# A planner that reckons TensorE's changes of array shape, and all first weights decoded in PSUM

## The chip, the cores and the metric

One core of one Trainium2 chip runs the whole kernel. The metric is the device time of one execution in microseconds (us), the median over several runs.

## The reference

Attention over 4 batches of 8 heads (576 tokens of 64 values) is followed by two feed-forward layers (512 to 2048 to 512) over the 2304 tokens, all in fp32. The attention has two parts that are added: one over pooled tokens (means of four), one local, in which a token sees the tokens at a distance under 4.

```python
def _attn_ref(q, k, v):
    q_d = q.reshape(B, H, Sd, factor, D).mean(axis=3)   # likewise k_d, v_d; factor = 4
    out_d = sm_attn(q_d, k_d, v_d)                      # softmax attention
    out_up = np.repeat(out_d, factor, axis=2)
    mask = np.abs(pos[:, None] - pos[None, :]) < factor
    scores = np.where(mask, scale * q @ k.T, -1e9)
    return out_up + softmax(scores) @ v

x = attn_out.transpose(0, 2, 1, 3).reshape(B * S, H * D)
h = x @ w_in;  x = (h * sigmoid(h)) @ w_out             # first layer
h = x @ w_in2; x = np.where(h > 0, h, np.exp(np.minimum(h, 0)) - 1) @ w_out2
```

## The kernel before

**Stages.** The kernel has an attention stage and a long feed-forward stage. Up to about 44 us TensorE works on batch 0's attention alone, in four pairs of heads. Then the first layer's first half of weights (8 slices of 128 hidden values, each a `w_in` and a `w_out` tile, so 16 weights, `i` from 0 to 15) is applied to the tokens in blocks of 256, as the GEMM units of `unit`: L1077 is the first product (x by `w_in`), L1125 the second (into the block's sums). The attention of batches 1 to 3 runs between these units. Blocks 0 and 1 are interleaved: slices 0 to 3 of block 0, of block 1, then slices 4 to 7 of each, so that both hold their sums at once. Block 2 needs batch 1's attention. Products of fp32 are made of three products of split values (high and low parts, `xh`, `xl`, `wh`, `wl`). Behind the attention stage `paired` runs the remaining passes as long streams of 128x384 and 128x512 products (L1453, L1541, L1543).

**The planner.** The order of instructions on every engine comes from a list scheduler that runs when the program is built. A `Job` has an engine, a duration in us, predecessors, a due time, PSUM banks that it takes (`Hold(banks, kind)`), and for TensorE a `mode`. `pick` finds the job that can start first; among the jobs of its engine that can start within `SLACK` (0.05 us) of it, it takes the one with the earliest due time. `emit` writes its instructions and moves the engine's clock. A job with an `other` engine is put on the one that ends it sooner, with a bias `PREFER`. The planner's durations are estimates; on the chip each engine runs its instructions in the planned order, and waits on semaphores where the plan was wrong. Before the change `STICK` is 0, so a job's shape plays no part, and `mode` knows only "t" (transposes) and "s" (small products); GEMM jobs have none.

**PSUM.** There are eight banks of 128x512 fp32. Kinds are "a" (attention), "h" (result of L1077), "y" (sums of a block, two banks each) and "w" (decoding of weights); at most 3 h, 6 of h and y together, and 2 of w are held at once (`bank_rule`).

**Decoding of a weight** (`decode_jobs`, called by `prepare`): weights land as 128x1024 32-bit words in a `ws` buffer, and come to be an fp32 tile `wf` in these steps: `first` (L411, ScalarE), `half` (L415, ScalarE), `second` (L419, a clamp, VectorE or GpSimd), `third` (L422, a shift and an OR, VectorE), `fourth` (L426, a merge of the sign, VectorE). For `i < N_PSUM` the value between these steps (`temp`) lies in a PSUM bank, else in `wf` itself. `prepare` then splits `wf` into a high part (L1054, ScalarE) and a low one (L1058, GpSimd).

```python
a = Job("A", 0.62, first, list(preds) + [landed[i]], takes=list(takes) + inner, uses=held)
b = Job("V", 0.70 if inner else 0.45, second, [a], other=None if inner or i >= 2 * FP else ("G", 1.1, lambda: second(nc.gpsimd)))
c = Job("V", VEC_[DM], third, [b, a2], port=not inner, uses=held)
```

**Attention** (`attend`, one call per batch and pair of heads): q and k are transposed (L635, full array), the local scores are 40 products of 64x64 (L747), the pooled scores 8 of 64x72 (L800), the pooled output 8 of 72x64 (L892), the local output 40 of 64x64 (L920 in two parts for batches 0 and 1, L958 for 2 and 3). Both softmax results are transposed for their products (L853, L874, "flips"). In the local softmax L766 takes the maxima, L771 subtracts and later scales (GpSimd), L861 copies flips out of PSUM; L839 scales the pooled one. For batch 0 the pooling of v is 44 products (L690). L1105 and L1106 are the first two steps behind a GEMM unit's first product.

**Products of zeros.** `filler` issues TensorE products of zeros (L356) at the start (`WARM`, nine) and, up to the first unit, into every planned gap of TensorE (`fill`). They write into the free bank that came free first.

Of the kernel before, what the change touches and what calls it, by code (L numbers as in the profile page):

```python
# [15 lines left out]
ALU = mybir.AluOpType  # L16
# [6 lines left out]
def attention_moe_moe2_kernel(ctx, tc, q, k, v, wi1, wo1, wi2, wo2, out):  # L23
    nc = tc.nc
# [3 lines left out]
    P = 128  # L28
# [15 lines left out]
    FP = NF // NPASS  # L44
# [8 lines left out]
    WIN = 64  # L53
    WARM = 9
    PREFER = {("G", "V"): 1.5, ("V", "G"): -1.5, ("A", "V"): 0.5, ("V", "A"): -0.5}
    PACKED, PE_POOLED, HALVED, CHUNKED, STICK, T_SECOND = 0, 1, 0, 4, 0.0, 40.0
    BACKLOG = 3.0
    D_ROWS, D_LOCAL, D_V, D_W, S_ROWS, S_LOCAL, X_AFTER = 1.6, 1.9, 1.5, 2.2, 1.1, 2.2, 1
    QUAD_FROM = 2
# [1 line left out]
    LEND = 1  # L61
    SOON, W_EARLY, W_AT = 9.0, 0, -3.0
    LATE, FRAC = 1.0, (0.25, 0.5, 0.75, 1.0)
    SLACK, MOST_H, N_PSUM, SPLIT_F = 0.05, 3, 8, 3
    T_MM, T_FIRST, T_PAIR = 0.1185, 46.0, 6.4
    LAG = 3
    ON_ACT = (0, 2, 3)
# [77 lines left out]
    now = [0.0]  # L145
# [56 lines left out]
    class Job:  # L202
# [61 lines left out]
        def emit(self):  # L264
            t = self.start()
            assert t is not None
            cand.remove(self)
            for h in self.takes:
                h.take()
            if self.eng == "P":  # L270
                if filling[0]:
                    fill(t)
                mode_of[0] = self.mode
                now[0] = t + self.dur
            self.fn()
            clock_of[self.eng] = t + self.dur
            if self.port:
                clock_of["port"] = t + self.dur
            self.end = t + self.dur + self.lat
            if self.dma is not None:  # L280
                clock_of["dma"] = max(clock_of["dma"], t + DMA_WAIT) + self.dma
                self.end = clock_of["dma"] + DMA_LAND + self.safe
            for h in self.uses:
                h.done(self)
            for j in self.after_me:
                j.open_ -= 1
                if not j.open_:
                    blocked.remove(j)
                    cand.append(j)
# [3 lines left out]
    def pick(limit=1e18):  # L293
        best = None
        for job in cand:
            s = job.start()
            if s is not None and s < limit:
                key = (s, job.due, job.serial)
                if best is None or key < best[0]:
                    best = (key, job)  # L300
        if best is None:
            return None
        s = best[0][0] + SLACK
        eng = best[1].eng
        ties = []
        for job in cand:
            if job.eng == eng or job.other and job.other[0] == eng:
                x = job.start()
                if x is not None and x <= s and job.eng == eng:
                    same = eng == "P" and job.mode is not None and job.mode == mode_of[0]  # L310
                    ties.append((job.due - (STICK if same else 0.0), job.serial, job))
        return min(ties)[2] if ties else best[1]

    def pump(t):
# [6 lines left out]
    def run(goals):  # L321
        goals = [j for j in goals if j.end is None]
        while goals:
            job = pick()
            assert job is not None, "stuck"
            job.emit()
            if job in goals:
                goals.remove(job)
# [22 lines left out]

    def filler(n):
        if n > 0:
            entry = min(banks.free, key=lambda x: x[:2])
            for _ in range(n):
                nc.tensor.matmul(entry[2], wz[0][:, :P], wz[0][:, :512], start=True, stop=True)  # L356

    def fill(t):
        gap = t - clock_of["P"]
        if banks.free:  # L360
            filler(min(int((gap - 0.1) / 0.22), 40))

    wz = []

# [26 lines left out]
    def decode_jobs(i, out, preds, takes=(), temp=None):  # L393

        def t():
            return (temp.tile.bitcast(I32) if temp is not None else out())

        def pairs_of(st):
            return st.rearrange("p (n w) -> p n w", w=2)

        held = []
        if i < 2 * FP:
            held = [Hold(WS)]
            wst[i] = held[0]
            landed[i] = Job("S", 0.55, lambda: load_w(i), [], takes=held, dma=D_W, safe=SAFE_W)
        else:
            landed[i] = Job("S", 0.55, lambda: load_w(i), [decoded[i - WS_N]] if i >= 2 * FP + WS_N else [decoded[n] for n in range(2 * FP)], dma=D_W, safe=SAFE_W)

        def first():
            st = pairs_of(wst[i])  # L410
            nc.scalar.activation(t().bitcast(F32), st[:, :, 1].bitcast(F32), AF.Abs, scale=65536.0)  # L411

        def half():
            st = pairs_of(wst[i])
            nc.scalar.activation(st[:, :, 0].bitcast(U32), st[:, :, 0].bitcast(U32), AF.Copy, scale=2.0 ** -29, bias=2.0 ** -10 - 0.5)  # L415

        def second(eng=nc.vector):
            tf = t().bitcast(F32)
            eng.tensor_scalar(tf, tf, 2.0, W_MAX, op0=ALU.max, op1=ALU.min)  # L419

        def third():
            nc.vector.scalar_tensor_tensor(t(), t(), 3, pairs_of(wst[i])[:, :, 0], op0=ALU.logical_shift_left, op1=ALU.bitwise_or)  # L422

        def fourth():
            st = pairs_of(wst.pop(i))
            nc.vector.scalar_tensor_tensor(out(), st[:, :, 1], -(1 << 31), t(), op0=ALU.bitwise_and, op1=ALU.bitwise_or)  # L426

        inner = [temp] if temp is not None else []
        a = Job("A", 0.62, first, list(preds) + [landed[i]], takes=list(takes) + inner, uses=held)
        a2 = Job("A", 0.66, half, [landed[i]], uses=held)  # L430
        b = Job("V", 0.70 if inner else 0.45, second, [a], other=None if inner or i >= 2 * FP else ("G", 1.1, lambda: second(nc.gpsimd)))
        c = Job("V", VEC_[DM], third, [b, a2], port=not inner, uses=held)
        d = Job("V", VEC_[DM], fourth, [c] + ([decoded[i - 1]] if i - 1 in decoded else []), port=not inner, uses=inner + held)
        decoded[i] = d
        return d
# [127 lines left out]
    def attend(i, due):  # L563
# [60 lines left out]
        for n_, cells in enumerate(([(0, c) for c in range(NTB - 1)], [(1, c) for c in range(NTB - 1)], [(0, NTB - 1), (1, NTB - 1)])):  # L624
            bank = Hold(banks, "a")

            def flip(cells=cells, bank=bank):
# [9 lines left out]
            used = {0: [hq], 1: [hk], 2: [hq, hk]}[n_]  # L637
            pj = Job(
                "P", 0.085 * len(cells), flip, [lq] if n_ == 0 else [lk] if n_ == 1 else [lq, lk], lat=0.2,
                takes=[bank] + ([hqk] if n_ == 0 else []), uses=used, mode="t",  # L640
            )
            pj.after(prior)
            prior = [pj]
# [38 lines left out]
        if by_pe:  # L682
# [9 lines left out]
                            start=n == 0, stop=n == len(POOLED_BY) - 1, skip_group_check=True,  # L692
                        )

            psv = Job("P", 1.3, pool_v, [lw], lat=0.2, takes=bankv, uses=[hw, hpool], mode="s")
            for j in range(2):
                dst = lambda j=j: hvd.tile[:HS, 2 * j * D:2 * (j + 1) * D]
                pv.append(alike(
# [30 lines left out]
        def follow(job, key):  # L729
            if key in chain:  # L730
                job.after([chain[key]])
            chain[key] = job
            return job

        for part, (s0, s1, halves_, outs) in enumerate(parts):
# [15 lines left out]
                            start=True, stop=True,  # L751
                        )

            psl = follow(Job("P", 0.15 + 0.11 * (s1 - s0) * 2, scores, copies, lat=0.2, takes=held + ([hE] if start_ else []), uses=[hqk], mode="s"), "psl")
            masked = []
            for j, bank in enumerate(held):
                def add_mask(j=j, bank=bank, s0=s0, s1=s1):
# [37 lines left out]
            def pooled_scores(halves_=halves_, bankd=bankd):  # L795
# [9 lines left out]
                        )  # L805

            psd = follow(Job(
                "P", 0.15 + 0.2 * len(halves_), pooled_scores, [red], lat=0.2, takes=bankd + ([hED, hsm] if start_ else []), uses=[hqkD], mode="s",
            ), "psd")
            exps = []  # L810
            for j, bank in enumerate(bankd):
# [36 lines left out]
            for g0, g1_ in groups:  # L848
# [5 lines left out]
                            bank.tile[:, (s - g0) * P:(s - g0 + 1) * P], E4(s, s + 1).rearrange("p s j w -> p (s j w)"), ident  # L854
                        )

                pj = follow(Job("P", 0.11 * (g1_ - g0), flip, [norm], lat=0.2, takes=[bank] + ([haT] if g0 == 0 else []), uses=[hE], mode="t"), "psE")
                n = (g1_ - g0) * P
                dst = lambda g0=g0, g1_=g1_: aT()[:, g0:g1_, :].rearrange("p s w -> p (s w)")
                flips[g0] = alike(  # L860
# [5 lines left out]
            for a in halves_:  # L866
# [6 lines left out]
                            y_ = x[:, c * HS:(c + 1) * HS] if by_pe else x.rearrange("p (m c) -> p c m", c=2)[:, c, :]  # L873
                            nc.tensor.transpose(bank.tile[:HS, (2 * j + c) * HS:(2 * j + c + 1) * HS], y_, ident[:HS, :HS])  # L874

                pj = follow(Job("P", 0.26, flip, [norm_d], lat=0.2, takes=[bank] + ([haD] if a == 0 else []), uses=[hED], mode="s"), "psD")
                dst = lambda a=a: aD()[:HS, :, a * HS:(a + 1) * HS]
                src = lambda bank=bank: bank.tile[:HS, :4 * HS].rearrange("p (n s) -> p n s", n=4)
                flips_d.append(alike(
# [14 lines left out]
                            start=(c == 0), stop=(c == 1),  # L894
                        )

            psu = follow(Job("P", 0.3 + 0.0015 * (m1 - m0), out_d, flips_d + pv, lat=0.2, takes=[banku], uses=[hvd, haD], mode="s"), "psu")
            ups = alike(
                0.19 + 0.0008 * (m1 - m0),
                lambda banku=banku, m0=m0, m1=m1: nc.scalar.activation(haD.tile[:, m0:m1], banku.tile[:, :m1 - m0], AF.Copy, scale=1.0 / FAC),  # L900
# [8 lines left out]
            if b < QUAD_FROM:  # L909
                for t in outs:  # L910
# [23 lines left out]
                            op=ALU.add,  # L934
                        )

                    pj = Job("P", 0.54, out_l, [lw] + [flips[g] for g in sorted(flips) if t == 1 or g == 0], lat=0.2, takes=[bank], uses=[hw, haT], mode="s")
                    end_ = due[t] if isinstance(due, tuple) else due + 0.5 * t
                    final.append(Job("V", 0.47, join, [pj, ups] + (sum(first_users.values(), []) if b == 1 else second_users if b else []), due=end_, uses=[bank, haD]))
                    x_written[pr, 2 * b + t] = final[-1]  # L940
# [21 lines left out]
                                start=True, stop=True,  # L962
                            )

            pj = follow(Job("P", 0.75, out_l, [lw] + [flips[g] for g in sorted(flips)], lat=0.2, takes=banko, uses=[hw, haT], mode="s"), "pso")
            for t, p0, p1 in ((0, 0, P), (1, 0, D), (1, D, P)):
                bank = banko[t]
                g0 = b * S + t * HALF
# [596 lines left out]
    with tc.manual_schedule():  # L1565
# [51 lines left out]

        for i in range(W_EARLY):
            landed[i].due = W_AT
        filler(WARM)  # L1620
        constants()
        pool_matrix()
# [2 lines left out]
        run(g1_jobs[0, 0])  # L1625
        run(g1_jobs[FILL_TO])
        filling[0] = False
        run([j for b_ in range(B) for j in batch_end[b_]] + list(kept_x.values()) + [x for p_ in w_split.values() for x in p_])
        PREFER.clear()
        attn_pools.close()  # L1630
# [73 lines left out]
```

## Time and profile before

| | |
|---|---|
| median of 3 runs | 893.6 us (892.75 to 894.23) |
| profiled execution, its own time | 893.9 us |
| its span, first to last instruction | 891.5 us |
| TensorE products busy | 875.7 us (98%) |
| VectorE, ScalarE, GpSimd busy | 673.1, 540.8, 273.0 us (76%, 61%, 31%) |
| mean granted clock of TensorE | 0.992 of full speed |

In the profile PE is TensorE's products, PEld its loads of weights, DVE VectorE, ACT ScalarE, POOL GpSimd, SP the engine that issues most DMAs. A busy PE includes the time that products wait in its pipeline. L1077 is line 1077 of the kernel. An operand is named by its tile: `b` is a PSUM bank, `wf` the decoded weight, `ws` its landing buffer, `ring`, `spare` and `yo` the attention's working tiles, `t` the value behind a unit's first product.

### The profile page before, as it was taken

The page shows a single profiled execution, that of the slowest core. Times are in us where ns is not written, and L with a number is a line of the kernel's source. Part 1 is how long each engine was busy: PE and PEld are TensorE (multiplying, and loading weights), DVE is VectorE, ACT ScalarE, POOL GpSimd, SP SyncE. Part 2 cuts the span into 40 slices and gives each one's busy share as a digit, 9 for nine tenths or more (in the row PEclk, how much of TensorE's full clock was granted, in tenths as well). Part 3 has the DMA queues.
Part 4 walks back from the last instruction along what each step waited for, and adds up shares of the span by engine and source line. Part 5 has one row for each costly group of instructions (what it writes and reads, how often), then busy time and mean ns, then how long its engine had stood idle before and what let it go on. Part 6 is the DMA issues. An engine that isn't in the chain of part 4 may idle for free.

```text
span 891.5 us, 17228 instructions
## 1 busy us (share of the span) xinstructions
PE 875.7 (98%) x6614; PEld 817.0 (92%) x6614; DVE 673.1 (76%) x1236; ACT 540.8 (61%) x1226; POOL 273.0 (31%) x278
## 2 busy tenths in 40 slices
PE   9989899999999999999999999999999999999998
PEld 6778798999999999999999999898898998998986
DVE  6899768786967988968848969489489888483562
ACT  4796546664547668648347477286497584571650
POOL 4687977875301211401014213001051031010000
PEclk9999899999999999999999999999999999999999
DMA  9896148551134345154432240350520430220301
GB/s 158 217 220 159 54 107 240 119 143 36 69 95 142 106 142 177 48 201 154 130 112 90 83 155 23 107 178 3 186 71 37 165 131 36 90 89 35 107 1 72
DMA packets 105522, 100.08 MB, mean 112 GB/s; under 512 B 62240, under 2 KB 92448, under 8 KB 105312
## 3 DMA queue, kind: packets, MB, share of 16 engines
q1 hardware_dynamic: 103072, 98.39, 37.2%
q8 instruction: 52, 0.85, 0.4%
q10 hardware_dynamic: 2368, 0.59, 0.4%
q14 instruction: 30, 0.25, 0.1%
HBM read 75.37 MB, written 23.59 MB: 111 GB/s over the span
## 4 chain that ended last, share of the span: by engine, by line
PE 90%; DVE 4%; POOL 2%; ACT 1%; DMA 1%; issue 1%; SPq 0%; POOLq 0%; DVEq 0%; ACTq 0%
PE b L1453 33%; PE b L1543 22%; PE b L1541 15%; PE b L1125 6%; PE b L1077 6%; PE b L635 1%; PE b L892 1%; PE b L920 1%; PE b L874 1%; PE b L800 1%; POOL w L1058 1%; PE b L853 1%; PE b L747 1%; DMA nat<-in_q_dram 1%; POOL wf L419 1%
## 5 line engine op out<-in xcount | busy, mean ns | idle before, releaser
L1543 PE MATMUL b<-w,grw 128*128 128x512 f32 x384 | 121.2, 389 | 0.0
L1543 PE MATMUL b<-w,ghk 128*128 128x512 f32 x288 | 99.1, 389 | 0.0
L1453 PE MATMUL b<-xhr,xaw 128*128 128x384 f32 x360 | 96.4, 335 | 0.0
L1541 PE MATMUL b<-grw,w 128*128 128x384 f32 x352 | 91.2, 334 | 0.0
L1543 PEld LDWEIGHTS b<-w,grw 128*128 128x128 f32 x384 | 72.1, 188 | 14.9
L1077 PE MATMUL b<-xh,w 128*128 128x256 f32 x384 | 84.5, 298 | 0.8 <-DVE t L1106 0.8
L1453 PE MATMUL b<-xhr,w 128*128 128x384 f32 x320 | 83.8, 335 | 0.0
L1125 PE MATMUL b<-gh,w 128*128 128x256 f32 x384 | 80.7, 292 | 0.0
L1543 PE MATMUL b<-w,glk 128*128 128x512 f32 x192 | 74.8, 389 | 0.0
L1541 PE MATMUL b<-ghk,w 128*128 128x384 f32 x248 | 71.6, 334 | 0.0
L1077 PEld LDWEIGHTS b<-xh,w 128*128 128x128 f32 x384 | 66.1, 198 | 2.2 <-DVE t L1106 1.2
L1235 POOL TENSOR_TENSOR w<-raw,w 128x512 fp32r<-128x512 f32 x16 | 22.8, 1435 | 144.9 <-ACT w L1233 129.8
L1453 PE MATMUL b<-xlr,xaw 128*128 128x384 f32 x200 | 66.9, 334 | 0.0
L1125 PEld LDWEIGHTS b<-gh,w 128*128 128x128 f32 x384 | 64.1, 193 | 1.5 <-issue 1.2
L1453 PEld LDWEIGHTS b<-xhr,xaw 128*128 128x128 f32 x360 | 65.4, 188 | 0.0
L1543 PEld LDWEIGHTS b<-w,ghk 128*128 128x128 f32 x288 | 54.1, 188 | 11.2
L1541 PEld LDWEIGHTS b<-grw,w 128*128 128x128 f32 x352 | 63.7, 188 | 0.0
L1465 ACT COPY hg<-b 128x384 f32<-128x384 f32 x60 | 28.5, 479 | 50.2 <-PE b L1453 49.2
L1453 PEld LDWEIGHTS b<-xhr,w 128*128 128x128 f32 x320 | 58.0, 188 | 0.2
L1236 DVE TENSOR_TENSOR xlr<-tail,xhr 128x768 fp32r<-128x768 f32 x51 | 49.6, 972 | 11.4 <-ACT xhr L1233 10.8
L1506 DVE SCALAR_TENSOR_TENSOR part<-b,part 128x384 f32<-128x384 f32 (+1 forms) x42 | 25.0, 608 | 43.2 <-PE b L1543 28.4
L1541 PE MATMUL b<-glk,w 128*128 128x384 f32 x168 | 56.1, 334 | 0.0
(262 smaller groups left out, 2443.2 us busy)
## 6 DMA issues: line engine op xcount, KB each, us to landing
ws<-in_moe_w_in_dram SPq DMA_DIRECT2D x32, 512.0 KB
ws<-in_moe_w_out_dram SPq DMA_DIRECT2D x31, 512.0 KB
tail<-x SPq DMA_DIRECT2D x24, 384.0 KB
x<-part SPq DMA_DIRECT2D x6, 768.0 KB
out_dram<-part SPq DMA_DIRECT2D x18, 256.0 KB
vw<-in_v_dram SPq DMA_DIRECT2D x28, 144.0 KB
tail<-xd SPq DMA_DIRECT2D x10, 384.0 KB
natv<-in_v_dram SPq DMA_DIRECT2D x22, 144.0 KB
```

The lines of the kernel that those rows point to most:

```text
L419: eng.tensor_scalar(tf, tf, 2.0, W_MAX, op0=ALU.max, op1=ALU.min)
L635: nc.tensor.transpose(bank.tile[:, n * TB:(n + 1) * TB], row(which, c)[:TB], ident[:TB, :TB])
L747: nc.tensor.matmul(held[j].tile[o:o + WIN, c:c + WIN], qT[j * D:(j + 1) * D, q0[w]:q0[w] + WIN], kT[j * D:(j + 1) * D, w0[w]:w0[w] + WIN], ...
L1077: nc.tensor.matmul(ph.tile[:, :NB0], w[a][:, c, :], x_slot(n, c, b_), start=start and m == 0, stop=stop and m == len(products) - 1,)
L1125: nc.tensor.matmul(y[d // 2].tile[:, o:o + NB0], w[m // 2][:, sl], gg(m % 2), start=f == 0 and m == 0 and d % 2 == 0, stop=fin and m == 2, ...
L1235: "G", GPS_[width], lambda: nc.gpsimd.tensor_tensor(lo(), src, hi().bitcast(F32), ALU.subtract), [a], due=due,
L1236: other=("V", VEC_[width], lambda: nc.vector.tensor_tensor(lo(), src, hi().bitcast(F32), ALU.subtract)),
L1453: nc.tensor.matmul(acc_, a[:, cs], b[:, c, :], start=fresh and c == 0 and m == 0, stop=c == 1 and m == 2, skip_group_check=True,)
L1465: snap[after, j] = [Job("A", ACT_[NB], lambda dst=dst, acc_=acc_: nc.scalar.copy(dst, acc_), [], gate, due=soon)]
L1506: nc.vector.scalar_tensor_tensor(dst, src, sc, dst, op0=ALU.mult, op1=ALU.add)
L1541: nc.tensor.matmul(y[d][:, :NB], wm[:, sl], gm, start=first, stop=last_)
L1543: nc.tensor.matmul(y[d], gm[:, sl], wm, start=first, stop=last_)
```

## The change

There are four parts. TensorE jobs get finer modes: none for everything on the full array (GEMM units, all transposes), "q" for 64x64 products, "d" for the pooled scores and the pooling of v, "u" for the pooled output, with new durations. `emit` adds 0.12 us to a TensorE job whose mode is not that of the job before (0.09 us if that had none), and `pick` moves the due time of a job with the mode at hand ahead by `STICK`, 3 us. All 16 first weights are decoded in PSUM, and the clamp has no way to GpSimd any more. The products of zeros have a bank of their own, from the start until the first unit's last L1077 job, and are issued whether or not another bank is free.

```diff
-    PACKED, ..., STICK, T_SECOND = 0, 1, 0, 4, 0.0, 40.0
+    PACKED, ..., STICK, T_SECOND = 0, 1, 0, 4, 3, 40.0
+    STICK_FROM = 0
-    SLACK, MOST_H, N_PSUM, SPLIT_F = 0.05, 3, 8, 3
+    SLACK, MOST_H, N_PSUM, SPLIT_F = 0.05, 3, 16, 3
...
+            dur = self.dur
             if self.eng == "P":
                 if filling[0]:
                     fill(t)
+                if self.mode != mode_of[0]:
+                    dur += 0.12 if mode_of[0] is not None else 0.09
                 mode_of[0] = self.mode
...
-                    same = eng == "P" and job.mode is not None and job.mode == mode_of[0]
-                    ties.append((job.due - (STICK if same else 0.0), job.serial, job))
+                    same = eng == "P" and job.mode == mode_of[0]
+                    ties.append((job.due - (STICK if same and s > STICK_FROM else 0.0), job.serial, job))
...
     def filler(n):
         if n > 0:
-            entry = min(banks.free, key=lambda x: x[:2])
             for _ in range(n):
-                nc.tensor.matmul(entry[2], wz[0][:, :P], wz[0][:, :512], start=True, stop=True)
+                nc.tensor.matmul(fill_bank.tile, wz[0][:, :P], wz[0][:, :512], start=True, stop=True)
     def fill(t):
         gap = t - clock_of["P"]
-        if banks.free:
-            filler(min(int((gap - 0.1) / 0.22), 40))
+        filler(min(int((gap - 0.1) / 0.22), 40))
+    fill_bank = Hold(banks, "f")
+    fill_bank.left = 1
...
-        b = Job("V", 0.70 if inner else 0.45, second, [a], other=None if inner or i >= 2 * FP else ("G", 1.1, lambda: second(nc.gpsimd)))
+        b = Job("V", 0.70 if inner else 0.45, second, [a])
...
-    psv = Job("P", 1.3, pool_v, ..., mode="s")                       # pooling of v, batch 0
+    psv = Job("P", 0.85, pool_v, ..., mode="d")
-    psl = follow(Job("P", 0.15 + 0.11 * (s1 - s0) * 2, scores, ..., mode="s"), "psl")
+    psl = follow(Job("P", 0.124 * (s1 - s0), scores, ..., mode="q"), "psl")
-    psd = follow(Job("P", 0.15 + 0.2 * len(halves_), pooled_scores, ..., mode="s"), "psd")
+    psd = follow(Job("P", 0.27 * len(halves_), pooled_scores, ..., mode="d"), "psd")
-    psu = follow(Job("P", 0.3 + 0.0015 * (m1 - m0), out_d, ..., mode="s"), "psu")
+    psu = follow(Job("P", 0.1 + 0.003 * (m1 - m0), out_d, ..., mode="u"), "psu")
-    pj = Job("P", 0.54, out_l, ..., mode="s")                        # batches 0 and 1
+    pj = Job("P", 0.6, out_l, ..., mode="q")
-    pj = follow(Job("P", 0.75, out_l, ..., mode="s"), "pso")         # batches 2 and 3
+    pj = follow(Job("P", 0.63, out_l, ..., mode="q"), "pso")
...
+        fill_bank.take()
         filler(WARM)
...
         filling[0] = False
+        fill_bank.done(g1_jobs[FILL_TO][-1])
```

The transposes of q and k, of the local and of the pooled softmax lose their `mode="t"` or `mode="s"` and have none.

## Rows read from the trace of the kernel before

**Rows 1.** Busy time by stretch: length, then PE, PEld, DVE, ACT, POOL, clock.

```profile
44.00:67.00 23.00, 18.76 (x257) 16.56 (x254) 22.40 (x46) 20.69 (x54) 19.85 (x22) 0.93 1.00 223
67.00:90.00 23.00, 21.63 (x243) 20.18 (x243) 22.00 (x36) 15.21 (x40) 17.11 (x17) 1.00 0.68 158
90.00:115.00 25.00, 21.56 (x174) 19.27 (x173) 16.70 (x26) 12.26 (x34) 21.41 (x17) 0.80 0.17 49
...
134.00:261.00 127.00, 126.62 (x1632) 120.07 (x1631) 97.88 (x215) 73.01 (x227) 69.81 (x85) 1.00 0.44 123
261.00:891.50 630.50, 626.88 (x3362) 592.61 (x3360) 467.84 (x814) 383.26 (x760) 104.43 (x80) 1.00 0.31 102
```

**Rows 2.** TensorE's waits: us in total, times, longest us.

```profile
PE b L853 <- DVE t L1106: 1.4, 1, 1.4
...
PE b L747 <- ACT spare L861: 0.9, 1, 0.9
```

**Rows 3.** TensorE in order of time, 98 to 105 us: start, us, idle before.

```profile
99.32 0.55 PE L853 MATMUL b<-ident,ring 128*128 128x128 f32 x3 [0.60 <-POOL ring L771]
...
102.75 0.50 PE L874 MATMUL b<-ident,ring 72*72 72x72 f32 x4 [1.16 <-POOL ring L839]
...
104.86 0.58 PE L1077 MATMUL b<-xh,w 128*128 128x256 f32 x1 [0.63 <-DVE t L1106]
```

**Rows 4.** Chain that ended last, 100 to 120 us: start, us, what.

```profile
104.86 2.93 PE b L1077 x12
...
108.94 2.86 PE b L1125 x12
...
117.84 1.44 PE b L1077 x12
```

**Rows 5.** GpSimd's groups of instructions, 0 to 135 us: count, busy us, mean ns.

```profile
L419 POOL TENSOR_SCALAR wf<-wf 128x512 f32<-128x512 f32 x6 | 13.0, 2162 | 2.2 <-ACT wf L411 2.2
```

**Rows 6.** VectorE's groups of instructions, 0 to 135 us.

```profile
L422 DVE SCALAR_TENSOR_TENSOR wf<-wf,ws 128x512 int32<-128x512 int32 x8 | 8.8, 1111 | 2.2 <-POOL wf L419 2.2
...
L426 DVE SCALAR_TENSOR_TENSOR wf<-ws,wf 128x512 int32<-128x512 int32 x8 | 6.8, 851 | 0.0
...
L419 DVE TENSOR_SCALAR b<-b 128x512 f32<-128x512 f32 x8 | 5.5, 694 | 1.4 <-ACT b L411 1.2
...
L422 DVE SCALAR_TENSOR_TENSOR b<-b,ws 128x512 int32<-128x512 int32 x7 | 4.7, 688 | 0.0
...
L419 DVE TENSOR_SCALAR wf<-wf 128x512 f32<-128x512 f32 x2 | 4.3, 2132 | 0.0
```

**Rows 7.** Line 419, 0 to 270 us: ns least/median/greatest, first and last start.

```profile
L419 DVE TENSOR_SCALAR raw<-raw x2: 420/424/428, 260.3 to 266.5; 128x512 f32<-128x512 f32 x2
```

**Rows 8.** TensorE in order of time, one attention pair in 171 to 176 us.

```profile
171.82 0.49 PE L874 MATMUL b<-ident,ring 72*72 72x72 f32 x4
172.15 0.38 PE L853 MATMUL b<-ident,ring 128*128 128x128 f32 x2
172.37 0.43 PE L874 MATMUL b<-ident,ring 72*72 72x72 f32 x4
172.61 0.36 PE L1077 MATMUL b<-xh,w 128*128 128x256 f32 x1
...
174.20 0.71 PE L892 MATMUL b<-ring,vd 72*64 72x144 f32 x8
174.84 0.81 PE L958 MATMUL b<-ring,vw 64*64 64x60 f32 x40
175.58 0.71 PE L800 MATMUL b<-qkD 64*72 64x144 f32 x8
```

**Rows 9.** Chain that ended last, 0 to 50 us.

```profile
27.36 1.57 PE b L690 x44
...
44.20 0.97 PE b L1077 x6
```

**Rows 10.** Chain that ended last, 118 to 160 us.

```profile
146.71 1.27 POOL ring L771
```

More of the change, by code (lines that the diff above doesn't have):

```diff
@@ L55, in attention_moe_moe2_kernel @@
     PREFER = {("G", "V"): 1.5, ("V", "G"): -1.5, ("A", "V"): 0.5, ("V", "A"): -0.5}
-    PACKED, PE_POOLED, HALVED, CHUNKED, STICK, T_SECOND = 0, 1, 0, 4, 0.0, 40.0
+    PACKED, PE_POOLED, HALVED, CHUNKED, STICK, T_SECOND = 0, 1, 0, 4, 3, 40.0
+    STICK_FROM = 0
     BACKLOG = 3.0
@@ L272, in emit @@
                     fill(t)
+                if self.mode != mode_of[0]:
+                    dur += 0.12 if mode_of[0] is not None else 0.09
                 mode_of[0] = self.mode
-                now[0] = t + self.dur
+                now[0] = t + dur
             self.fn()
-            clock_of[self.eng] = t + self.dur
+            clock_of[self.eng] = t + dur
             if self.port:
-                clock_of["port"] = t + self.dur
-            self.end = t + self.dur + self.lat
+                clock_of["port"] = t + dur
+            self.end = t + dur + self.lat
             if self.dma is not None:
@@ L415, in half, with second @@
             nc.scalar.activation(st[:, :, 0].bitcast(U32), st[:, :, 0].bitcast(U32), AF.Copy, scale=2.0 ** -29, bias=2.0 ** -10 - 0.5)
-        def second(eng=nc.vector):
+        def second():
             tf = t().bitcast(F32)
-            eng.tensor_scalar(tf, tf, 2.0, W_MAX, op0=ALU.max, op1=ALU.min)
+            nc.vector.tensor_scalar(tf, tf, 2.0, W_MAX, op0=ALU.max, op1=ALU.min)
         def third():
@@ L639, in attend @@
                 "P", 0.085 * len(cells), flip, [lq] if n_ == 0 else [lk] if n_ == 1 else [lq, lk], lat=0.2,
-                takes=[bank] + ([hqk] if n_ == 0 else []), uses=used, mode="t",
+                takes=[bank] + ([hqk] if n_ == 0 else []), uses=used,
             )
@@ L693, in pool_v @@
                         )
-            psv = Job("P", 1.3, pool_v, [lw], lat=0.2, takes=bankv, uses=[hw, hpool], mode="s")
+            psv = Job("P", 0.85, pool_v, [lw], lat=0.2, takes=bankv, uses=[hw, hpool], mode="d")
             for j in range(2):
@@ L752, in scores @@
                         )
-            psl = follow(Job("P", 0.15 + 0.11 * (s1 - s0) * 2, scores, copies, lat=0.2, takes=held + ([hE] if start_ else []), uses=[hqk], mode="s"), "psl")
+            psl = follow(Job("P", 0.124 * (s1 - s0), scores, copies, lat=0.2, takes=held + ([hE] if start_ else []), uses=[hqk], mode="q"), "psl")
             masked = []
@@ L807, in attend @@
             psd = follow(Job(
-                "P", 0.15 + 0.2 * len(halves_), pooled_scores, [red], lat=0.2, takes=bankd + ([hED, hsm] if start_ else []), uses=[hqkD], mode="s",
+                "P", 0.27 * len(halves_), pooled_scores, [red], lat=0.2, takes=bankd + ([hED, hsm] if start_ else []), uses=[hqkD], mode="d",
             ), "psd")
@@ L855, in flip @@
                         )
-                pj = follow(Job("P", 0.11 * (g1_ - g0), flip, [norm], lat=0.2, takes=[bank] + ([haT] if g0 == 0 else []), uses=[hE], mode="t"), "psE")
+                pj = follow(Job("P", 0.11 * (g1_ - g0), flip, [norm], lat=0.2, takes=[bank] + ([haT] if g0 == 0 else []), uses=[hE]), "psE")
                 n = (g1_ - g0) * P
@@ L874, in flip @@
                             nc.tensor.transpose(bank.tile[:HS, (2 * j + c) * HS:(2 * j + c + 1) * HS], y_, ident[:HS, :HS])
-                pj = follow(Job("P", 0.26, flip, [norm_d], lat=0.2, takes=[bank] + ([haD] if a == 0 else []), uses=[hED], mode="s"), "psD")
+                pj = follow(Job("P", 0.26, flip, [norm_d], lat=0.2, takes=[bank] + ([haD] if a == 0 else []), uses=[hED]), "psD")
                 dst = lambda a=a: aD()[:HS, :, a * HS:(a + 1) * HS]
@@ L895, in out_d @@
                         )
-            psu = follow(Job("P", 0.3 + 0.0015 * (m1 - m0), out_d, flips_d + pv, lat=0.2, takes=[banku], uses=[hvd, haD], mode="s"), "psu")
+            psu = follow(Job("P", 0.1 + 0.003 * (m1 - m0), out_d, flips_d + pv, lat=0.2, takes=[banku], uses=[hvd, haD], mode="u"), "psu")
             ups = alike(
@@ L935, in join @@
                         )
-                    pj = Job("P", 0.54, out_l, [lw] + [flips[g] for g in sorted(flips) if t == 1 or g == 0], lat=0.2, takes=[bank], uses=[hw, haT], mode="s")
+                    pj = Job("P", 0.6, out_l, [lw] + [flips[g] for g in sorted(flips) if t == 1 or g == 0], lat=0.2, takes=[bank], uses=[hw, haT], mode="q")
                     end_ = due[t] if isinstance(due, tuple) else due + 0.5 * t
@@ L963, in out_l @@
                             )
-            pj = follow(Job("P", 0.75, out_l, [lw] + [flips[g] for g in sorted(flips)], lat=0.2, takes=banko, uses=[hw, haT], mode="s"), "pso")
+            pj = follow(Job("P", 0.63, out_l, [lw] + [flips[g] for g in sorted(flips)], lat=0.2, takes=banko, uses=[hw, haT], mode="q"), "pso")
             for t, p0, p1 in ((0, 0, P), (1, 0, D), (1, D, P)):
```

## The prediction

> **What bounds the kernel now.** I read the table by stages first [rows 1]; its columns are the stretch, the busy time and count of PE, PEld, DVE, ACT and POOL, the granted clock of TensorE, the share of the DMA engines and GB/s. From 261 us on TensorE has 626.88 us of work in 630.5, and from 134 to 261 us 126.62 in 127; the planner's edits touch nothing behind 261 us, and in 134 to 261 us time can come only out of TensorE's own work. The idle time lies ahead: 4.24 us in 44 to 67 us, 1.37 in 67 to 90, and 3.44 (25.00 - 21.56) in 90 to 115 us. In that last stretch the granted clock is 0.80 on average, and POOL is busy for 21.41 of 25 us while the DMA engines are at 0.17: it is POOL, not the loads, that the stage runs on.
>
> Second, TensorE's idle time by releaser and in order of time [rows 2, 3]. The one wait of 1.4 us on `t` (L1106) is the whole idle time of 67 to 90 us. In 98 to 105 us TensorE waits five times, 3.44 us together, for POOL (the subtraction of the maxima L771, the scaling L839), for copies behind them, and for L1106 on DVE. Right behind these gaps the clock falls to 1.2 GHz: twelve matmuls of the first GEMM take 2.93 us, twelve of the second 2.86, where twelve take 1.44 at 2.4 GHz [rows 4].
>
> Third, what POOL and DVE do there [rows 5, 6]. Weights 8 to 15 are decoded in SBUF. The planner thinks the clamp `second` takes 1.1 us on POOL; six of them took 2.16 us each, 13.0 us together. The two that stayed on DVE took 2.13 us each, and the two steps after it took 1.11 and 0.85 us on average. For weights 0 to 7, whose intermediate lies in a PSUM bank, the same steps took 0.69 us each. So in SBUF the two engines hold each other up, in PSUM not.
>
> **The change part by part.**
>
> *Decode in PSUM (N_PSUM 16).* POOL loses 13.0 us [rows 5]. DVE did 2 clamps, 8 shifts and 8 merges for weights 8 to 15 in 4.3 + 8.8 + 6.8 = 19.9 us; as PSUM forms, 8 x 0.694 + 16 x 0.688 = 16.6 us (the merge taken at the shift's price): DVE has 3.3 us less to do although it takes over six clamps [rows 6]. What this frees on TensorE's path: the idle 3.44 us of 90 to 115 us; the 1.37 us of 67 to 90 us, which stood behind a DVE that was at 22.00 of 23 us with a stretched clamp in front; and the half clock. For the last, the matmuls of [rows 4] give 1.49 + 1.42 = 2.9 us at the least, and 0.20 of the clock over 25 us 5.0 us at the most; attention work between them ran slow too, so I take 4.4. Together 9.2 us. As the waits of 98 to 105 us are those of an attention chain that has no GEMM beside it, I leave 1.5 us of them in place (bounds 0 and 7.8): 7.7 us.
>
> One row speaks against PSUM: with nothing in its way a clamp from SBUF to SBUF takes 0.424 us on DVE [rows 7], and 0.694 in PSUM [rows 6]. The Trainium skill says why, in VectorE: DVE Perf Modes, "Why PSUM operands drop a tier": an operand in PSUM shuts the mode that needs both SBUF read ports, so the fp32 clamp falls to the plain rate. This trace agrees, by 0.694 against 0.424; what it would make of the time is the last rival. My sum has the dearer price in it already.
>
> *A bank for each decode.* A decode holds a bank for at least its clamp, shift and merge, 3 x 0.69 = 2.1 us [rows 6], eight times: 16.6 bank-us, while blocks 0 and 1 hold four banks with their sums. Nothing here shows it for that stretch. Below: 0, if a bank is always free. Above: 16.6 us, if each hold stood on TensorE's path. The nearest row is 44 to 67 us, where the first weights were decoded in PSUM: TensorE waited 0.9 us for a bank that ACT was still reading (L747 on L861) [rows 2]. It had four sums fewer there, so I take 1.5 us lost.
>
> *The shape rule (STICK 3, 0.12 us per change).* The step from 64x64 products to flips costs 0.33 us for four flips [rows 8] (171.82 to 172.15), and four with no change ahead of them 0.24 (172.37 to 172.61): 0.09 us per change. One attention pair has six changes: into the scores L747 (ahead of 171.82), out of them, into L892, L958, L800 and out again [rows 8]. Twelve pairs run beside the GEMMs, so the changes are worth 12 x 6 x 0.09 = 6.5 us, the most that could go. The least is below nothing: a preference can move an urgent job 3 us back in the order, worth at worst one such wait, 1.4 us [rows 2]. If the scores of one pair meet the products L958 of another, two changes go per pair; I take it for the eight pairs of batches 2 and 3, where TensorE has a queue of ready work: 8 x 2 x 0.09 = 1.4 us. The new durations (scores 1.25 to 0.62 us, products 0.75 to 0.63) agree with the 0.74 us that each takes with its change [rows 8]: the order is planned on truer numbers, for which I book nothing.
>
> *The front (a bank for the products of zeros).* Until the first GEMM at 44.20 us [rows 9] seven banks are left instead of eight, and batch 0 has four pairs in flight. A product of zeros no longer needs a free bank, so all planned gaps are filled. The pooling products are now planned at 0.85 + 0.12 us and take 1.57 [rows 9]: four times 0.60 us by which TensorE is late where the planner sees a gap to fill. Bounds: 2.4 us lost, and 1.4 won as the bank that a product of zeros overwrites is never in use (the size of one wait for a bank, [rows 2]). I take 0.5 lost.
>
> Sum: 7.7 + 1.4 - 1.5 - 0.5 = 7.1 us. The profiled execution took 893.9 us, 2.4 more than its span of 891.5, and stands 0.3 over the median of 893.6. 893.9 - 7.1 = 886.8 us.
>
> **The rivals.**
> - *Only the decode acts.* The due times lie further apart than 3 us, or TensorE has one ready job at a time, and the shape rule changes no order. For it: the changes lie among GEMM units that are due every 2 us or so. Then 893.9 - 7.7 + 1.5 + 0.5 = 888.2 us.
> - *Given back at block 2.* Block 2 needs batch 1's attention whole. The chain that ended last runs through POOL's L771 at 146.71 us [rows 10], inside the attention that comes between: a TensorE that arrives 7 us earlier would find x not written. Against it: in 134 to 261 us POOL is busy for 69.81 of 127 us, DVE for 97.88, so both can come earlier too, and TensorE idled 0.38 us there. Then 893.5 us or so, no change that can be measured: 0.2% of 893.6 is 1.8 us, about what a measurement of this kernel tells from none.
> - *Slower: banks.* With four sums, two banks of h and two decodes all eight are held; attention takes a bank 14 times per pair. If in the two pairs that run while four sums are held half of the takes wait for half a decode and its queue, 1.0 us, that is 14 us of delay in a chain. TensorE's own gain is 7.7 + 1.4 = 9.1; once more than 9.1 us of it can't be covered by GEMM work, the kernel is slower. With nearly all of it bare, 893.9 - 9.1 + 13 = 897.8 us.
> - *DVE becomes the bound.* It is at 22.00 of 23 us in 67 to 90 us [rows 1]; if it stays the engine that TensorE waits for, the difference of 0.27 us is paid eight times, 2.2 us: 889.0. Its chance is small: the clamp from SBUF took 2.13 us on DVE in this stretch [rows 6], not 0.42. (This is the outcome by the rule of the Trainium skill, VectorE: DVE Perf Modes, named above.)
>
> **How the numbers follow.** Chances: forecast 0.46, only the decode 0.18, DVE the bound 0.06, given back 0.11, banks 0.19. The first three are faster: 0.70; same 0.11; slower 0.19. The forecast's own range: all of the 9.2 us and two thirds of the changes of shape (4.3 us) won, nothing given back, gives 880.4; half of the 9.2 us left in place, no change of shape saved, banks and front as taken (893.9 - 4.6 + 2.0) gives 891.3. The range for 8 in 10 starts at 880 and reaches to 897, which leaves out the dearer half of the slower case and the rarest of the good ones.
>
> **What would show it.** Right: no clamp on POOL; shifts and merges of all sixteen weights near 0.69 us; idle time in 90 to 115 us under 2 us, and clock 1.00 there; runs of 64x64 products of two pairs side by side; the long pieces of L1453 in the chain some 7 us earlier. Wrong: TensorE waiting for banks (ACT or DVE as releaser of a `b`) in 67 to 125 us, a first GEMM well behind 44.20 us [rows 9], or a new gap ahead of block 2.

## The result and the profile after

The changed kernel takes 885.86 us (885.2 to 886.4, 4 runs) against 893.37 us (892.75 to 894.23, 4 runs) before: ratio 0.9915, 95% interval 0.9898 to 0.9932, some 7.5 us faster. 886.8 was predicted, in a range of 880 to 897. Its span is 883.5 us against 891.5. Its lines stand four lower in the file: the clamp is L423, the shift L426, the merge L430, the first product of a unit L1081, the second L1129, the scores L751, the long products L1457.

Busy time by stretch of the changed kernel, the columns of [rows 1]:

```profile
44.00:67.00 23.00, 20.66 (x257) 17.84 (x256) 20.23 (x40) 18.16 (x48) 19.59 (x23) 0.85 1.05 231
67.00:90.00 23.00, 22.13 (x244) 20.36 (x244) 19.28 (x39) 17.92 (x46) 19.45 (x23) 1.00 0.56 158
90.00:115.00 25.00, 25.00 (x320) 23.68 (x319) 17.95 (x37) 16.90 (x51) 19.40 (x23) 1.00 0.31 84
...
134.00:261.00 127.00, 126.80 (x1589) 120.84 (x1586) 94.31 (x210) 73.24 (x215) 65.02 (x79) 1.00 0.38 108
261.00:883.50 622.50, 618.90 (x3304) 584.66 (x3302) 462.24 (x805) 377.71 (x749) 104.38 (x80) 1.00 0.31 102
```

TensorE's idle time in 90 to 115 us has gone from 3.44 us to none and the clock from 0.80 to 1.00; in 67 to 90 us the idle time is 0.87 instead of 1.37. In 44 to 67 us TensorE idles 2.34 us instead of 4.24, but its clock is 0.85 instead of 0.93. POOL's 21.41 us in 90 to 115 have become 19.40, for 23 instructions instead of 17.

VectorE's decode in the changed kernel, 0 to 135 us, answers [rows 6]: count, busy us, mean ns.

```profile
L423 DVE TENSOR_SCALAR b<-b 128x512 f32<-128x512 f32 x16 | 10.9, 688 | 1.6 <-ACT b L415 1.4
L426 DVE SCALAR_TENSOR_TENSOR b<-b,ws 128x512 int32<-128x512 int32 x15 | 10.4, 693 | 0.4
L430 DVE SCALAR_TENSOR_TENSOR wf<-ws,b 128x512 int32<-128x512 int32 x15 | 10.1, 672 | 0.1
```

All sixteen clamps now run on DVE at the price of the first eight, shifts and merges too (the sixteenth of each has a lent buffer and stands in a row of its own).

How far this carries is seen where the stage ends, in the chain that ended last: the first piece of the long products, of the kernel before and of the changed one.

```profile
261.15 1.04 PE b L1453 x6
```

```profile
253.17 1.04 PE b L1457 x6
```

7.98 us earlier, against 8.0 us of span: nothing is given back behind the attention stage. What the stage still loses shows in TensorE's order of time, 54 to 62 us of the changed kernel (answers [rows 3]):

```profile
55.18 0.39 PE L1081 MATMUL b<-xl,w 128*128 128x256 f32 x1 [0.47 <-POOL xl L1027]
...
55.52 0.58 PE L639 MATMUL b<-ident,nat 96*128 96x96 f32 x5
55.88 0.36 PE L1081 MATMUL b<-xh,w 128*128 128x256 f32 x1
57.08 0.38 PE L1081 MATMUL b<-xl,w 128*128 128x256 f32 x1 [0.83 <-POOL xl L1027]
...
59.18 1.03 PE L639 MATMUL b<-ident,spare 96*128 96x96 f32 x5 [0.16 <-DMA spare<-in_q_dram]
...
61.53 0.58 PE L1081 MATMUL b<-xh,w 128*128 128x256 f32 x1
```

The first units wait for x's low parts, which POOL makes late; then five transposes take 1.03 us where they took 0.58 shortly before, and a first product 0.58 instead of 0.36: TensorE is at 1.2 GHz (granted clock 0.50) from about 58.8 to about 65.6 us.

### The profile page after: what moved, and what is told of

It reads as the page before. It is cut to its first block, busy times and chain, and to the rows that moved or that the text cites. A ratio compares the mean times of both kernels' runs of the same rounds, so it can differ in the third digit from the quotient of the medians.

```text
span 883.5 us, 17302 instructions
## 1 busy us (share of the span) xinstructions
PE 873.5 (99%) x6631; PEld 815.6 (92%) x6631; DVE 659.7 (75%) x1238; ACT 542.1 (61%) x1224; POOL 265.1 (30%) x284
## 4 chain that ended last, share of the span: by engine, by line
PE 95%; DMA 2%; DVE 1%; POOL 1%; ACT 0%; issue 0%; SPq 0%; DVEq 0%; POOLq 0%; ACTq 0%
PE b L1457 33%; PE b L1547 22%; PE b L1545 15%; PE b L1081 8%; PE b L1129 8%; PE b L639 2%; PE b L751 1%; PE b L804 1%; PE b L857 1%; PE b L896 1%; PE b L878 1%; PE b L924 1%; PE b L359 1%; DMA nat<-in_q_dram 1%; PE b L962 1%; PE b L694 1%
## 5 line engine op out<-in xcount | busy, mean ns | idle before, releaser
L1457 PE MATMUL b<-xhr,xaw 128*128 128x384 f32 x360 | 96.4, 335 | 0.0
L1545 PE MATMUL b<-grw,w 128*128 128x384 f32 x352 | 91.2, 334 | 0.0
L1081 PE MATMUL b<-xh,w 128*128 128x256 f32 x384 | 83.5, 295 | 0.9 <-ACT w L1058 0.5
L1457 PE MATMUL b<-xhr,w 128*128 128x384 f32 x320 | 83.8, 335 | 0.0
L1129 PE MATMUL b<-gh,w 128*128 128x256 f32 x384 | 79.2, 288 | 0.0
L1545 PE MATMUL b<-ghk,w 128*128 128x384 f32 x248 | 71.6, 334 | 0.0
L1081 PEld LDWEIGHTS b<-xh,w 128*128 128x128 f32 x384 | 64.8, 193 | 2.5 <-issue 0.6
L1457 PE MATMUL b<-xlr,xaw 128*128 128x384 f32 x200 | 66.9, 334 | 0.0
L1457 PEld LDWEIGHTS b<-xhr,xaw 128*128 128x128 f32 x360 | 65.5, 188 | 0.0
L1129 PEld LDWEIGHTS b<-gh,w 128*128 128x128 f32 x384 | 63.2, 191 | 0.6 <-issue 0.4
L1545 PEld LDWEIGHTS b<-grw,w 128*128 128x128 f32 x352 | 63.7, 188 | 0.0
L1457 PEld LDWEIGHTS b<-xhr,w 128*128 128x128 f32 x320 | 58.0, 188 | 0.2
L1545 PE MATMUL b<-glk,w 128*128 128x384 f32 x168 | 56.1, 334 | 0.0
```

Source lines behind the costliest of these rows:

```text
L1081: nc.tensor.matmul(ph.tile[:, :NB0], w[a][:, c, :], x_slot(n, c, b_), start=start and m == 0, stop=stop and m == len(products) - 1,)
L1129: nc.tensor.matmul(y[d // 2].tile[:, o:o + NB0], w[m // 2][:, sl], gg(m % 2), start=f == 0 and m == 0 and d % 2 == 0, stop=fin and m == 2, ...
L1457: nc.tensor.matmul(acc_, a[:, cs], b[:, c, :], start=fresh and c == 0 and m == 0, stop=c == 1 and m == 2, skip_group_check=True,)
L1545: nc.tensor.matmul(y[d][:, :NB], wm[:, sl], gm, start=first, stop=last_)
```

## The experiments

Ratios are to the kernel before, from runs beside it on the same chip. "Changes" are TensorE's changes of array shape from 44 us to the first long product, counted product by product in order of time, with 128x128, 96x128 and 72x72 taken as one shape, the full array. The expectations' count is lower by one for the changed kernel (79).

| run | us | ratio (95%) | clamps on GpSimd | changes |
|---|---|---|---|---|
| before | 892.53 to 893.82 | 1 | 6 | 82 |
| changed | 885.86 | 0.9915 (0.9898 to 0.9932) | 0 | 80 |
| changed, again | 885.77 | 0.9914 (0.9898 to 0.9930) | 0 | 80 |
| decode alone | 886.14 | 0.9926 (0.9907 to 0.9945) | 0 | 76 |
| all but the decode | 892.43 | 0.9995 (0.9981 to 1.0008) | 6 | 83 |
| no preference | 886.75 | 0.9928 (0.9909 to 0.9946) | 0 | 79 |
| old bank of zeros | 888.02 | 0.9940 (0.9921 to 0.9959) | 0 | 78 |
| clamp on VectorE, SBUF | 890.24 | 0.9963 (0.9947 to 0.9978) | 0 | 79 |
| clamp's price 2.16 | 885.43 | 0.9913 (0.9898 to 0.9927) | 3 | 77 |
| all clamps on GpSimd | 899.93 | 1.0071 (1.0054 to 1.0088) | 8 | 78 |
| seven banks | 890.97 | 0.9974 (0.9961 to 0.9987) | 0 | 82 |
| longer filling | 884.98 | 0.9907 (0.9892 to 0.9923) | 0 | 75 |
| three prices | 886.75 | 0.9933 (0.9909 to 0.9958) | 0 | 85 |
| prices and filling | 887.30 | 0.9933 (0.9916 to 0.9950) | 0 | 78 |

**Which part makes the gain: the decode alone.** On the kernel before:

```diff
-    SLACK, MOST_H, N_PSUM, SPLIT_F = 0.05, 3, 8, 3
+    SLACK, MOST_H, N_PSUM, SPLIT_F = 0.05, 3, 16, 3
-        b = Job("V", ..., second, [a], other=None if inner or i >= 2 * FP else ("G", 1.1, lambda: second(nc.gpsimd)))
+        b = Job("V", ..., second, [a])
```

> The kernel before with one part of the change: all sixteen weights decoded in PSUM, no clamp on GpSimd. Theory (the decode makes the gain): 886 to 888.5 us, no idle time of TensorE over 1 us in 90 to 115 us, granted clock there 1.00. Rival (the shape rule and its truer durations make it): 891 us or more, with waits for banks in 67 to 125 us that the truer plan had avoided.

Ratio 0.9926, within the interval of the whole change. Its stretches from 44 to 115 us, and its clamps:

```profile
44.00:67.00 23.00, 19.19 (x250) 16.87 (x248) 21.72 (x45) 20.28 (x53) 19.06 (x22) 0.85 1.00 207
67.00:90.00 23.00, 21.28 (x208) 19.73 (x207) 18.19 (x36) 16.25 (x43) 17.84 (x23) 1.00 0.73 183
90.00:115.00 25.00, 25.00 (x317) 23.99 (x317) 17.02 (x37) 16.58 (x48) 19.70 (x22) 1.00 0.31 75
```

```profile
L419 DVE TENSOR_SCALAR b<-b x16: 675/689/700, 31.9 to 100.3; 128x512 f32<-128x512 f32 x16
```

No idle time and full clock in 90 to 115 us, and no clamp over 0.700 us. So the decode, that is PSUM and no way to GpSimd together, makes the gain.

**All but the decode.** The changed kernel with the removed lines above put back.

> The changed kernel with the old decode: weights 8 to 15 in SBUF, the clamp free to go to GpSimd. Theory (the decode): 891 to 894 us, clamps of over 1.9 us on GpSimd, a half-clock stretch of 5 us or more between 90 and 120 us. Rival (shape rule): 888 us or less.

Ratio 0.9995: the new modes, prices, preference and bank of zeros together move nothing that shows in an interval of 0.9981 to 1.0008. The idle time is back in 90 to 115 us (2.59 us, at a clock of 0.93, which is some 3.5 us at half speed and not the expected 5), and so are the clamps on POOL:

```profile
90.00:115.00 25.00, 22.41 (x275) 20.55 (x276) 19.95 (x34) 15.27 (x39) 23.64 (x20) 0.93 0.38 98
```

```profile
L423 POOL TENSOR_SCALAR wf<-wf x6: 1910/1919/2347, 73.1 to 110.7; 128x512 f32<-128x512 f32 x6
```

**No preference.** On the changed kernel:

```diff
-    PACKED, ..., STICK, T_SECOND = 0, 1, 0, 4, 3, 40.0
+    PACKED, ..., STICK, T_SECOND = 0, 1, 0, 4, 0.0, 40.0
```

> The changed kernel with a preference of 0 us for the shape at hand; modes, 0.12 us per change and new durations stay. Theory (the rule moves few changes: 82 shape changes behind 44 us before, 79 after, 0.09 us each, so 0.3 us): 885 to 887.5 us, over 79 changes. Rival (the rule is worth 1.4 us or more): 887.5 us or more, with 95 changes or more.

886.75 us, as the theory said: 79 changes without the preference, 80 with it, and intervals that overlap. The preference does not do what it says: TensorE's changes of shape are as many with it, and the kernel with the decode alone, which knows nothing of shapes, has fewer than either, 76.

**Old bank of zeros.** On the changed kernel, the lines of `filler` and `fill` as before, `fill_bank` gone.

> The changed kernel with the products of zeros in whichever bank came free first, and none where no bank is free. Theory (off the path: the first unit started at 43.91 us with the bank and at 44.20 without): 885 to 887 us. Rival (seven banks in the front cost the 0.5 us that was booked, or more): 885 us or less, with a first unit before 43.4 us.

888.02 us, over what the theory allowed, and the rival (a gain) is out too. Its profile is of the shortest of its six executions (885.84 us) and does not show where the others lose: the first unit starts at 46.16 us instead of 43.91, and yet the long products at 253.24 us, near the 253.01 with the bank of zeros. Its interval touches that of the changed kernel, so whether a bank of its own is worth some 2 us stays open; a cost of it does not show.

**Where the clamp runs, and where its value lies.** On the kernel before, VectorE alone, but in SBUF:

```diff
-        b = Job("V", 0.70 if inner else 0.45, second, [a], other=None if inner or i >= 2 * FP else ("G", 1.1, lambda: second(nc.gpsimd)))
+        b = Job("V", 0.70 if inner else 0.45, second, [a])
```

> The kernel before with the clamp of weights 8 to 15 kept on VectorE, but still from SBUF to SBUF. Theory A (GpSimd's 13 us of clamps starved TensorE; where the value lies does not matter): 886 to 888 us, as with the decode in PSUM. Theory B (both engines hold each other up over SBUF, wherever the clamp runs): 889 to 892 us, with shifts and merges in SBUF at 0.8 us or more on average.

890.24 us: less than half of the gain, in theory B's range, with shifts of 0.82 and merges of 0.79 us on average. The clamps of this run (ns least/median/greatest) and its stretch of 90 to 115 us:

```profile
L419 DVE TENSOR_SCALAR wf<-wf x8: 408/1144/4030, 70.7 to 105.5; 128x512 f32<-128x512 f32 x8
```

```profile
90.00:115.00 25.00, 22.80 (x246) 20.73 (x246) 22.73 (x38) 16.13 (x43) 18.24 (x18) 0.93 0.40 106
```

The same clamp takes 0.41 us where GpSimd does nothing beside it (at 83.78 and 105.54 us), and 4.030 at worst. DVE is busy for 22.73 of 25 us, against 17.02 with the same clamps in PSUM. The longest clamp ends behind four instructions that GpSimd runs one after the other:

```profile
98.89 4.03 DVE L419 TENSOR_SCALAR wf<-wf 128x512 f32<-128x512 f32 x1
```

```profile
98.34 1.14 POOL L839 TENSOR_TENSOR ring<-ring,small 72x576 f32<-72x576 f32 x1
99.44 1.25 POOL L771 TENSOR_TENSOR ring<-ring,small 128x640 f32<-128x640 f32 x1
100.66 0.72 POOL L1111 TENSOR_TENSOR gl<-t,gh 128x256 fp32r<-128x256 f32 x1
101.35 1.28 POOL L1058 TENSOR_TENSOR w<-wf,w 128x512 fp32r<-128x512 f32 x1
```

The Trainium skill (SBUF — State Buffer, "Who interferes with whom") says that VectorE and GpSimd share a pair of SBUF ports that one of them holds for a whole instruction. This run agrees that a clamp in SBUF can stand until GpSimd is done, but the wait spans four instructions and not one. In the run with the decode alone the clamps in PSUM took 0.700 us at most.

**Is it the wrong price?** On the kernel before, one number:

```diff
-        ... ("G", 1.1, lambda: second(nc.gpsimd)))
+        ... ("G", 2.16, lambda: second(nc.gpsimd)))
```

> The kernel before with the planner's price of a clamp on GpSimd set from 1.1 to the measured 2.16 us; nothing else. Theory C (the wrong price misled the order): 887 to 890 us, with three clamps or fewer left on GpSimd. Theories A and B (the clamp's own load or the contention): with several clamps still on GpSimd 891 to 894 us.

885.43 us, ratio 0.9913, better than theory C's 887 to 890: this one number brings as much as the whole change. The planner now leaves three clamps on POOL, at 70.8, 92.7 and 108.8 us, and puts five on DVE (ns least/median/greatest):

```profile
L419 DVE TENSOR_SCALAR wf<-wf x5: 408/477/1484, 73.7 to 101.0; 128x512 f32<-128x512 f32 x5
L419 POOL TENSOR_SCALAR wf<-wf x3: 1909/1909/1925, 70.8 to 108.8; 128x512 f32<-128x512 f32 x3
```

```profile
90.00:115.00 25.00, 24.27 (x297) 22.19 (x287) 24.78 (x47) 17.76 (x50) 20.91 (x17) 1.00 0.52 146
```

This profile is of the longest of its five executions, 887.31 us. DVE is at its end here, 24.78 of 25 us, and TensorE idles only 0.73 us all the same, at full clock. So PSUM isn't needed for the gain. The price can have acted through the order of everything, or by taking clamps off POOL; the next run keeps the true price and puts the clamps back on POOL.

**All clamps on GpSimd, at the true price.** On the kernel before:

```diff
+        b = Job("V", 0.70, second, [a]) if inner or i >= 2 * FP else Job("G", 2.16, lambda: second(nc.gpsimd), [a])
```

> The kernel before with the clamps of weights 8 to 15 all put on GpSimd, at the measured price of 2.16 us: more load there than before (8 clamps instead of 6), but a plan that knows it. Theory C (the wrong price misled the order): 885 to 888.5 us. Theory A (the load of the clamps on GpSimd): 891 us or more, with TensorE waiting for GpSimd in 90 to 115 us.

899.93 us, 0.7% slower than before. Its clamps on POOL, its stretches, and TensorE's longest waits behind 67 us:

```profile
L419 POOL TENSOR_SCALAR wf<-wf x8: 1912/1916/2454, 69.5 to 113.1; 128x512 f32<-128x512 f32 x8
```

```profile
90.00:115.00 25.00, 20.69 (x258) 19.11 (x259) 22.30 (x40) 15.39 (x43) 20.70 (x17) 0.91 0.45 123
115.00:134.00 19.00, 15.64 (x118) 14.11 (x118) 7.23 (x15) 8.27 (x20) 14.02 (x16) 0.76 0.14 32
```

```profile
PE b L874 <- POOL ring L839: 3.3, 1, 3.3
PE b L920 <- ACT ws L415: 2.0, 1, 2.0
```

The wait of 3.3 us for POOL ends at 125.09 us, behind the 90 to 115 us that the expectation named; in these TensorE waits for ACT and DVE. A plan that knows the price does not help if all eight clamps are on POOL. Theory C falls in the form "the order alone". That the price mattered because it kept clamps off POOL fits these runs but is argued: six clamps on POOL at the true price were not run.

**Seven banks.** On the changed kernel, `fill_bank.done(...)` moved to the end of the attention stage, so that the bank stands empty from 44 us on.

> The changed kernel with the bank of the products of zeros kept (unused) to the end of the attention stage: seven banks for everything from 44 us on. Theory (banks are short with two sums, h and decodes, 1.5 us booked): 888 to 893 us, with new waits of TensorE for banks behind 67 us. Rival (banks do not bind): 885 to 887 us.

890.97 us: one bank fewer costs 0.6%, about 5 us. TensorE's longest waits in 44 to 135 us of this run:

```profile
PE b L1081 <- DVE wf L430: 1.3, 1, 1.3
...
PE b L639 <- DVE wf L430: 0.8, 1, 0.8
PE b L1081 <- DVE t L1110: 0.6, 1, 0.6
```

L639 waits for a merge, which makes a value it does not read and frees a bank that it writes: a wait for a bank that a decode held. The wait of 1.3 us is of the same kind; it ends at 97.04 us and is all the idle time of 90 to 115 us, so there is a new wait for a bank behind 67 us, as the theory said. Yet this is the smaller part of the 5 us: the first long product starts at 255.08 us, 2.1 us behind the changed kernel's 253.01, and from there to the end the run takes 633.5 us instead of 630.5. The other 3.0 us are lost at 360 to 370 us, where the long passes wait for weights that are being split, as the changed kernel's never do. TensorE's waits behind 252 us:

```profile
PE b L1545 <- DVE w L1240: 0.7, 3, 0.3
PE b L1545 <- ACT w L1237: 0.3, 1, 0.3
```

So a bank is worth some 2 us in the attention stage; why its lack makes those weights late, 100 us behind that stage, is open.

**Longer filling.** On the changed kernel, products of zeros from a small tile of their own go on to block 0's fourth unit; 36 of them come to stand in 52.3 to 62.7 us, fewer than expected.

```diff
+                if late_fill[0]:
+                    z = zeros_late.bitcast(BF16)
+                    for e in range(4):
+                        nc.tensor.matmul(fill_bank.tile[:, e * P:(e + 1) * P], z, z, start=True, stop=True)
+                    continue
...
-        run(g1_jobs[FILL_TO])
+        late_fill[0] = True
+        run(g1_jobs[0, 3])
```

> The changed kernel with products of zeros (small ones, from a tile of their own) in TensorE's planned gaps up to the fourth unit of block 0 instead of the first, some 60 small products more; their bank is held as long. Theory (the stretch at 1.2 GHz in 58 to 65.6 us costs about 3 us and can be kept away): 882 to 885 us, clock 1.00 in 44 to 67 us. Rival (the gaps are not where the plan sees them, and the products of zeros stand before real work): 886 to 889 us.

```profile
44.00:67.00 23.00, 20.74 (x286) 18.10 (x286) 20.66 (x41) 18.40 (x48) 20.07 (x24) 1.00 1.05 224
```

The clock is 1.00 in 44 to 67 us instead of 0.85, and the time 884.98 us, ratio 0.9907 against 0.9915: the expected 882 to 885 us was just met, but the step from the changed kernel is within both intervals. The first long product comes at 252.45 us instead of 253.01, but in the repetition of the changed kernel (below) at 252.14. The clock's theory holds, its 3 us do not.

**Other prices, and both together.** On the changed kernel, in the second run with the longer filling:

```diff
-            psv = Job("P", 0.85, pool_v, ...
+            psv = Job("P", 1.45, pool_v, ...
-            smr = Job("V", 0.22, invert, exps)
+            smr = Job("V", 0.47, invert, exps)
-                pv.append(alike(1.2, halves, 0.68, whole, ...
+                pv.append(alike(1.2, halves, 1.06, whole, ...
```

> The changed kernel with three more durations set to what the trace shows: pooling products of v 0.85 to 1.45 us, the two steps on the sums of the pooled softmax 0.22 to 0.47, the sum over v rows on VectorE 0.68 to 1.06. Theory C carried on (true prices make a better order): 882.5 to 885 us, with a shorter stretch at 1.2 GHz in 44 to 67 us. Rival (these stand beside other work): 885 to 887.5 us.

> The three durations and the longer filling with products of zeros together, on the changed kernel. If both help and add up: 881.5 to 884 us, clock 1.00 in 44 to 67 us. If neither does: 885 to 887 us.

The changed kernel beside them:

> The changed kernel as it is, once more, as the yardstick for the runs beside it: 884.5 to 887 us.

885.77 us for it, as expected; 886.75 us for the prices alone, so the rival, though the stretch at 1.2 GHz is shorter, as the theory said (clock 0.93 in 44 to 67 us). Both together take 887.30 us, against either expectation. Yet the first long product of that run starts at 251.50 us, ahead of the changed kernel's 253.01 and its repetition's 252.14, and the clock in 44 to 67 us is 1.00. TensorE's waits behind 252 us, of which the changed kernel has none:

```profile
PE b L1552 <- DVE w L1247: 0.9, 1, 0.9
PE b L1552 <- ACT w L1244: 0.9, 1, 0.9
```

The lead is lost there: from the first long product to the end the run takes 632.9 us instead of 630.5, and 1.8 of these 2.4 us are waits for the splitting of the next layer half's weights (L1552 is the second product of the long passes). That is no sign that the later stage can take no more lead: the run with seven banks waits at the same place (its L1545), though it comes there later than the changed kernel. What makes these weights late in two of the runs stays open.

## Why the prediction was right, step by step

**The frame held.** The time came out of 44 to 134 us and passed through: 7.98 us at the first long product, 8.0 in the span. "Given back at block 2" did not happen; the one lead that was given back (prices and filling) was lost at about 360 us, not at block 2.

**Decode, 7.7 us of 9.2: right in size, in part by luck.** Alone it brings 0.74%, 6.6 us. In its profile the idle time of 67 to 115 us went from 4.81 to 1.72 us, and 0.20 of the clock over 25 us, 5.0 us, came back, 8.1 us together. The remnant of 1.5 us that I left in place in 98 to 105 us is not there; instead 44 to 67 us lost 1.8 us by a clock of 0.85 for 0.93, which the prediction did not have. The two misses nearly cancel.

**"So in SBUF the two engines hold each other up, in PSUM not": right of the durations, too much said of the cause.** The prices came out as taken (0.688 us for the clamp, 0.693 for the shift). But the run with one price changed has five clamps in SBUF and three on POOL and is as fast. What fits all runs is that TensorE is starved by clamps on POOL, planned at 1.1 and taking 2.16 us: with eight there it is 0.7% slower, with three or none 0.6 to 0.9% faster (seven banks apart), except where all eight go to DVE through SBUF and wait for POOL's own work (0.37% faster). For that exception the cause is argued, from the clamp of 4.03 us and DVE's 22.73 busy us; no run takes it apart. PSUM is one of two ways to that.

**Shape rule, 1.4 us: the term that was mis-sized; it measured 0.** A change costs 0.09 us, as read: four flips behind the scores took 0.33 us in all five places of the kernel before, and 0.24 in five behind other flips. But the rule saves 2 of 82, 0.2 us, and none against the run without it. The rival "only the decode acts" was the true description; I had given it 0.18. Its time, 888.2, is 2.3 us over the measured 885.86 mostly because of the next two terms.

**Banks, 1.5 us lost: 0.9 at most.** Behind 67 us the changed kernel shows 0.5 us behind L430 and 0.4 behind L884. The worry had its ground (a whole bank fewer costs 2 us in this stage and 3 behind it), but eight holds of some 2 us did not add up to a bank. **Front, 0.5 us lost: none lost.** The first unit came 0.3 us earlier.

**DVE as the bound:** DVE was busy for 19.28 of 23 us in 67 to 90 us, where it had been 22.00, and for 17.95 of 25 in 90 to 115, where it had been 16.70; it did not become the bound. And where it was busy for 24.78 of 25 (the priced clamp), the kernel was as fast.

Two losses of 2.0 us together that hardly came and a gain of 1.4 us that wasn't there nearly cancel, which is why 886.8 came so near: that nearness is luck. What was right is the stage, the decode as the main term, and nothing given back.

## What to carry to other kernels

In a kernel whose order is planned with estimated durations, compare the plan's price of each operation with its measured duration, and first where the loaded engine is an alternative of another: one wrong price of 1.1 for 2.16 us was worth as much as the whole change. That price moved work off a starved engine; three other prices put right moved nothing that could be measured. Before a part of a larger change gets the credit, run it alone and run the rest without it, which here took two runs.

## What the runs showed of the hardware that had not been expected

- GpSimd takes 1.91 us for a clamp of 128x512 at its least, and 1.28 us on average for a subtraction of two operands of that size (L1058 of the kernel before; 1.31 in the run with eight clamps): the operation with less to read is the slower one.
- On VectorE the same clamp from SBUF to SBUF took from 0.408 to 4.030 us, the longest behind four GpSimd instructions in a row; in PSUM it took from 0.675 to 0.700.
- With 36 products of zeros between 52.3 and 62.7 us TensorE's granted clock stayed at 1.00 in 44 to 67 us, where both profiles of the changed kernel have 0.85; the time that this gave back was within the noise.
